# Token sums and split y made ahead one operation a step, parked in DRAM and read back on GpSimd's queue; the low half of h one projection later

## The chip, the cores and the metric

The kernel runs on one core of a Trainium2 chip. The metric is device time in microseconds (us). The engines are called PE (TensorE, the matmuls), PEld (its weight loads), DVE (VectorE), ACT (ScalarE), POOL (GpSimd) and SP (SyncE, which here issues DMAs).

## What is computed

The reference, cut to what matters. Attention with random features comes first; two MLPs follow, and the change lies in these alone.

```python
x = attention(q, k, v, omega)            # 4 x 576 tokens -> x of 2304 x 512
# kind 1 (SwiGLU), d_ff = 1536
xn = x / rms(x) * rms_g
x = (silu(xn @ w_gate) * (xn @ w_val)) @ w_out
# kind 2, d_ff = 2048
x = silu(x @ w_in) @ w_out2
```

The weights come in as 64-bit floats, read as pairs of 32-bit words.

## The kernel before

Tokens lie in five blocks: 0 to 3 of 512, block 4 of 256. Every fp32 operand is kept as a high and a low half in the fast matmul type (fp32r): ACT writes the high half (a copy), DVE the low half (operand minus high), and each product is three matmul passes (high x high, high x low, low x high). xs[j] holds the split activations of block j, in four chunks of 128 channels; ya[j] its sums y in fp32; a `w_tile` slot holds a split weight.

The hidden dimension is cut into f-blocks of 128, 12 in kind 1 and 16 in kind 2. Blocks 0, 1 and 4 are done in **sweeps** of two f-blocks each: `g1_glu` (kind 1) projects gate and value, multiplies them (L254), and `split_h` makes the two halves of h (L224 on ACT, L225 on DVE); `g2_glu` adds the y product to ya (L285, L296) while the next block's projections run. `n1` is the last kind-1 sweep, `n2` the last of kind 2. In kind 2 `g1_mlp` has one projection and no product, and `g2_mlp` (L318, sums L329) makes y.

Blocks 2 and 3 are done in **quads**, by a scheme that takes 7 block products in place of 8 (L483), 10 quads of one f-block in kind 1 and 8 of two in kind 2. They need four sums of token blocks, T1 to T4, split and laid into parts of xs: T1 and T2 in xs[0], T3 in xs[1], T4 in xs[3], which are free once the sweeps have been through. They need sums of weight blocks too (`sums`, L442 to L445), and splits of those (`pieces`, `split`, low half at L359). `pieces` for quad k+1 and `out_pieces` for quad k's output weight go out during quad k, one group of at most two operations a step, from the list `todo`. Kept fp32 weights come back from DRAM by `load` and `load_out`.

Before the quads of a kind, the T work (`t_value`, L377; low half at L359, high at L401) goes out in the last sweep, after `flush` has emptied the list; POOL does T3 in kind 1. After the last kind-1 quad, `split_y` writes the y of blocks 0 and 1, split, to xs[0] and xs[1] for kind 2 (ACT L562, DVE L359), while the last `both` (y of blocks 2 and 3) runs: its own splits stand at L275.

The weights are prepared along the way: `Prep.tick` loads one weight (L155 to L166 are five DVE operations, L169 two POOL additions, L173 ACT's high half, L176 DVE's low half), and `need` ticks on until a weight is there. The lists of weights to prepare are extended in `hook`, per sweep.

Code runs in the order in which `stream` yields steps; each engine has its own queue and takes its instructions in that order. SP issues the DMAs in order too.

Of the kernel before, what the change touches and what calls it, by code (L numbers as in the profile page):

```python
# [20 lines left out]
def kernel(  # L21
# [345 lines left out]
    def t_value(kind, nm, k, eng):  # L367


        def b(r, c):  # L370
# [1012 lines left out]
```

## Time and profile before

| | us |
|---|---|
| median of 3 runs (1035.70 to 1037.78) | 1036.72 |
| profiled execution | 1036.71 |
| span in the profile | 1034.6 |
| PE busy | 1000.7 |
| DVE busy | 775.7 |
| ACT busy | 438.2 |
| POOL busy | 352.9 |

The profile is of one execution; times in it count from the start of the span. The mean granted clock of the span was 0.985 of 2.4 GHz. Where the granted clock of a stretch is below 1.00, PE ran a part of it at 1.2 GHz. An operation's time in a timeline is its own duration; the distance from one start to the next on an engine is shorter where operations overlap by some hundredths.

### The profile page before, as it was taken

To read this page: it belongs to the slowest core of one execution; us is meant where nothing else is said; L and a number is where in the kernel's file an instruction comes from. 1 tells how busy PE (TensorE), PEld (TensorE's weight loads), DVE (VectorE), ACT (ScalarE), POOL (GpSimd) and SP (SyncE) were. 2 spreads that over 40 slices of the span, in tenths; PEclk is the share of its full clock that TensorE was granted. 3 is DMA by queue.
4 is the path that set the end of the run, shared out by engine and by line. 5 is a ranking of instruction groups with operands and counts; after the bars stand their busy time and mean duration, and the time that the engine had idled before them with its cause. 6 is when DMAs were issued, how large, how long until landed. Compare 5 with 4: busy or idle time off the path is not lost.

```text
span 1034.6 us, 14957 instructions
## 1 busy us (share of the span) xinstructions
PE 1000.7 (97%) x5315; PEld 850.4 (82%) x5315; DVE 775.7 (75%) x1579; ACT 438.2 (42%) x991; POOL 352.9 (34%) x365
## 2 busy tenths in 40 slices
PE   8999999999999999988999987999999998999998
PEld 7999998888888888776888765788888886788877
DVE  6899999534767768887777875799977658576675
ACT  6888886433222212134332334433323235533441
POOL 7656644312434434512122230545434302121100
PEclk9999999999999999988999998999999999999999
DMA  7353221212425324101111230444433213221102
GB/s 186 100 156 91 75 62 43 92 37 76 123 92 150 95 92 137 38 21 61 52 41 61 84 121 1 122 148 129 151 112 107 89 41 102 63 69 52 41 21 82
DMA packets 86586, 88.33 MB, mean 85 GB/s; under 512 B 27632, under 2 KB 64752, under 8 KB 86512
## 3 DMA queue, kind: packets, MB, share of 16 engines
q1 hardware_dynamic: 86512, 87.38, 28.2%
q8 instruction: 42, 0.69, 0.3%
q14 instruction: 32, 0.26, 0.1%
HBM read 66.39 MB, written 20.97 MB: 84 GB/s over the span
## 4 chain that ended last, share of the span: by engine, by line
PE 80%; DVE 14%; ACT 4%; issue 2%; DMA 0%; SPq 0%; DVEq 0%; ACTq 0%
PE g L231 22%; PE y L318 17%; PE g L483 11%; PE y L285 10%; PE b L906 5%; PE b L231 3%; PE kv L989 3%; PE b L1034 2%; DVE s L377 2%; PE b L887 2%; PE b L1261 2%; PE b L1020 1%; DVE h L225 1%; DVE w L359 1%; DVE s L362 1%
## 5 line engine op out<-in xcount | busy, mean ns | idle before, releaser
L169 POOL TENSOR_TENSOR m<-m,raw 128x512 int32<-128x512 int32 x136 | 188.9, 1389 | 315.6 <-DVE m L166 304.0
L231 PE MATMUL g<-xs,w 128*128 128x512 f32 (+1 forms) x1392 | 276.4, 356 | 8.3 <-DVE s L254 6.1
L231 PEld LDWEIGHTS g<-xs,w 128*128 128x128 f32 x1392 | 232.2, 191 | 48.2 <-DVE s L254 6.3
L318 PE MATMUL y<-w,h 128*128 128x512 f32 (+1 forms) x870 | 207.7, 395 | 8.0 <-ACT h L224 4.4
L318 PEld LDWEIGHTS y<-w,h 128*128 128x128 f32 x870 | 163.9, 191 | 46.1 <-ACT h L224 5.2
L225 DVE TENSOR_TENSOR h<-s,h 128x512 fp32r<-128x512 f32 (+1 forms) x134 | 102.7, 774 | 115.7 <-ACT h L224 115.6
L483 PE MATMUL g<-xs,w 128*128 128x512 f32 x756 | 182.4, 400 | 6.9 <-DVE s L362 5.3
L483 PEld LDWEIGHTS g<-xs,w 128*128 128x128 f32 x756 | 144.1, 192 | 42.6 <-DVE s L362 8.1
L285 PE MATMUL y<-h,w 128*128 128x512 f32 (+1 forms) x648 | 138.5, 370 | 3.0 <-DVE ya L296 2.8
L285 PEld LDWEIGHTS y<-h,w 128*128 128x128 f32 x648 | 112.9, 190 | 25.5 <-DVE ya L296 4.7
L224 ACT ACTIVATE h<-s 128x512 fp32r<-128x512 f32 (+1 forms) x134 | 78.0, 587 | 120.7 <-DVE s L254 77.3
L329 DVE TENSOR_TENSOR ya<-y,ya 128x512 f32<-128x512 f32 (+1 forms) x127 | 84.4, 681 | 21.3 <-PE y L318 20.9
L173 ACT ACTIVATE w<-m 128x512 fp32r<-128x512 f32 x68 | 43.0, 632 | 130.3 <-POOL m L169 130.2
L442 POOL TENSOR_TENSOR w<-w 128x256 f32<-128x256 f32 x18 | 15.9, 884 | 238.2 <-DMA w<-kept1v 91.4
L945 ACT ACTIVATE e<-b,nb 128x128 f32<-128x128 f32 x272 | 77.5, 386 | 8.8 <-DVE nb L934 8.5
L176 DVE TENSOR_TENSOR w<-m,w 128x512 fp32r<-128x512 f32 x68 | 67.8, 997 | 4.2 <-ACT w L173 4.0
L296 DVE TENSOR_TENSOR ya<-y,ya 128x512 f32<-128x512 f32 (+1 forms) x100 | 60.4, 630 | 14.0 <-PE y L285 14.0
L906 PE MATMUL b<-bd,hl 128*128 128x256 f32 x432 | 69.5, 299 | 0.4 <-DVE hl L896 0.3
L362 DVE TENSOR_TENSOR s<-s,g 128x512 f32<-128x512 f32 x90 | 61.3, 681 | 9.7 <-PE g L483 9.2
L359 DVE TENSOR_TENSOR w<-w,w 128x512 fp32r<-128x512 f32 (+1 forms) x98 | 65.6, 683 | 0.6 <-ACT w L455 0.5
L906 PEld LDWEIGHTS b<-bd,hl 128*128 128x128 f32 x432 | 56.9, 194 | 1.7 <-DVE hl L896 0.6
L921 DVE TENSOR_REDUCE small<-b 128x4 f32<-128x512 f32 x72 | 50.1, 695 | 5.8 <-PE b L906 3.3
(96 smaller groups left out, 1131.0 us busy)
## 6 DMA issues: line engine op xcount, KB each, us to landing
raw<-in_moe_w_out_dram SPq DMA_DIRECT2D x28, 512.0 KB, 4.0
raw<-in_moe_w_in_dram SPq DMA_DIRECT2D x16, 512.0 KB, 4.2
raw<-in_moe_w_gate_dram SPq DMA_DIRECT2D x12, 512.0 KB, 4.0
raw<-in_moe_w_val_dram SPq DMA_DIRECT2D x12, 512.0 KB, 4.0
x<-in_k_dram SPq DMA_DIRECT2D x16, 256.0 KB, 3.3
va<-in_v_dram SPq DMA_DIRECT2D x32, 128.0 KB, 3.3
x<-in_q_dram SPq DMA_DIRECT2D x16, 256.0 KB, 3.0
kept2i<-m SPq DMA_DIRECT2D x16, 256.0 KB, 4.2
```

The lines of the kernel that those rows point to most:

```text
L169: tt(out=mi, in0=mi, in1=(low if step == 5 else high).bitcast(I32), op=ALU.add)
L224: nc.scalar.activation(out=ht[:, 0, :], in_=s, func=AF.Copy)
L225: nc.vector.tensor_tensor(out=ht[:, 1, :], in0=s, in1=ht[:, 0, :].bitcast(F32), op=ALU.subtract)
L231: nc.tensor.matmul(out=ps, lhsT=w[:, a, cc * P:(cc + 1) * P], rhs=xs[j][:, c, cc, :], start=(n == 0), stop=(n == 3 * KC - 1),)
L285: nc.tensor.matmul(out=ps, lhsT=wt[1, "o", f][:, a, d * P:(d + 1) * P], rhs=hs[f][:, c, :], start=(n == 0), stop=(n == nn - 1),)
L318: nc.tensor.matmul(out=ps, lhsT=hs[f][:, a, t * P:(t + 1) * P], rhs=wt[2, "p", f][:, c, d0:d1], start=(n == 0), stop=(n == nn - 1),)
L329: nc.vector.tensor_tensor(out=o[:, t, d0:d1], in0=ps, in1=o[:, t, d0:d1], op=ALU.add)
L359: nc.vector.tensor_tensor(out=out, in0=a, in1=b, op=ALU.subtract)
L362: nc.vector.tensor_tensor(out=out, in0=a, in1=b, op=ALU.add)
L483: nc.tensor.matmul(out=ps, lhsT=self.t[n][:, w, o:o + P], rhs=rhs(b, c)[:, k, :], start=start and m == 0 and k == 0, stop=stop and m == 2 ...
L906: nc.tensor.matmul(out=st.ps[:, 2 * j:2 * j + 2, :].rearrange("p h m -> p (h m)"), lhsT=st.hl[:, c, j, :], rhs=bd[:, a, :], start=(n == 0) ...
L945: nc.scalar.activation(out=st.e[:, h, :], in_=st.ps[:, h, :], func=AF.Exp, bias=st.nb[:, h:h + 1])
```

## The change

What it does:

- `split_h` gives ACT its copy and puts DVE's low subtract in a list, `owed`; `settle` issues it after the next projection.
- T1, T2 and T3 are computed in an earlier sweep (sweep 2 of kind 1 by its number, n1 + 2 of kind 2, and the one behind it), one operation a step on DVE, split into a weight slot and written to DRAM by SP (`park`); `t_load` reads them into xs in the last sweep, with DMAs issued on POOL's queue. T4 is written directly.
- `split_y` is gone. `y_jobs` splits one chunk of ya[0] or ya[1] in each of the quads 1 to 8, parks it, and `y_load` reads all eight back on POOL's queue after quad 9 (512 KB each).
- The weight sums go from POOL to DVE.
- `pieces` are given out in two lists with the next `load` between them; `out_pieces` of quad 0 go ahead with the first pieces; the ring of output slots has three entries in place of four.
- In kind 2, silu of z comes before the y stretch and not after it.
- A low half of the fourth chunk that `g2_glu` wrote in the last kind-1 sweep, with no high half to it (L275), is left out.
- The weights of sweep n1 + 2 are added to the list after the last kind-1 quad, not in sweep n1 + 1.

The core of the diff:

```diff
 def split_h(s, j):
     nc.scalar.activation(out=ht[:, 0, :], in_=s, func=AF.Copy)
-    nc.vector.tensor_tensor(out=ht[:, 1, :], in0=s, in1=ht[:, 0, :].bitcast(F32), op=ALU.subtract)
+    owed.append(lambda: nc.vector.tensor_tensor(
+        out=ht[:, 1, :], in0=s, in1=ht[:, 0, :].bitcast(F32), op=ALU.subtract
+    ))
     return ht
+def settle():
+    while owed:
+        owed.pop(0)()
 ...
     yield from proj(wt[1, "g", f], j, p)
+    settle()
 ...
+def park(key, slot, value):
+    t, v = [], []
+    def high():
+        v.append(value())
+        t.append(w_tile(*slot))
+        nc.scalar.activation(out=t[0][:, 0, :], in_=v[0], func=AF.Copy)
+    def low():
+        dsub(t[0][:, 1, :], v[0], t[0][:, 0, :].bitcast(F32))
+        parked[key] = cache.tile([P, 2, TB * P], F32, name="parked_%s%d%d" % key)
+        nc.sync.dma_start(out=parked[key], in_=t[0].bitcast(F32))
+    return [high, low]
+def unpark(key, out):
+    nc.gpsimd.dma_start(out=out, in_=parked[key])
+def t_load(kind, *names):
+    for nm in names:
+        j, h = RHS[nm]
+        for k in range(2):
+            unpark((nm, kind, k), xs[j][:, :, 2 * h + k, :])
+def y_load():
+    for j in (0, 1):
+        for d in range(KC):
+            unpark(("y", j, d), xs[j][:, :, d, :])
 ...
-    self.oslots = [[(1, 7), (1, 8), (1, 4), (1, 5)][k % 4]]
+    self.oslots = [[(1, 7), (1, 8), (1, 4)][k % 3]]
 ...
 def sums(self):
-    tt = nc.gpsimd.tensor_tensor
+    tt = nc.vector.tensor_tensor
 ...
 def hook(si, j, n):
+    if si == (2 if kind == 1 else n1 + 2):
+        todo.extend(t_jobs(kind, ((1, 6), (1, 7), (1, 8)) if kind == 1 else ((1, 8), (1, 7), (1, 5))))
 ...
     if at == (0, 0):
+        flush(todo)
         q.load()
         q.load_out()
     elif at == (0, 1):
-        jobs = [e for k in range(2) for nm in ("T1", "T2") for e in t_jobs(kind, nm, k, vec)]
-        todo.extend(groups(jobs) + groups(q.pieces() + [quads[kind, 1].load]))
+        t_load(kind, "T2", "T1")
+        a, b = q.pieces()
+        todo.extend(groups(a + [quads[kind, 1].load] + b + q.out_pieces()))
     elif at == (1, 1):
-        flush(todo)
-        ...
+        t_load(kind, "T3")
 ...
+    jobs = [lambda: None] * (4 if pend else 0)
     if k + 1 < count:
-        jobs += quads[kind, k + 1].pieces()
-    if k + 2 < count:
-        jobs.append(quads[kind, k + 2].load)
-    jobs += q.out_pieces()
+        a, b = quads[kind, k + 1].pieces()
+        jobs += a + ([quads[kind, k + 2].load] if k + 2 < count else []) + b
+    if k:
+        jobs += q.out_pieces()
     ...
+    if k and ys:
+        a, b = ys.pop(0)
+        todo += [[a], [b]]
 ...
-    if kind == 1:
-        pend = along(pend, [[lambda j=j, d=d: split_y(j, d)] for j in (0, 1) for d in range(KC)])
+    if kind == 2:
+        settle()
+    else:
+        prep.jobs += prep_list(n1 + 2)
+        y_load()
```

How DVE's row reads in sweep 3 of kind 1, block 0, before: L254 is the product of gate and value, L225 the low half of h, L176 a weight's low half, L155 to L166 the decoding of another weight, L296 a y sum.

```order
L254 TENSOR_TENSOR s<-s,g 128x512
L225 TENSOR_TENSOR h<-s,h 128x512
L176 TENSOR_TENSOR w_5_4538<-m_4493,w_5_4538 128x512
L155 TENSOR_SCALAR m_4577<-raw_4540 128x512
L158 TENSOR_SCALAR raw_4540<-raw_4540 128x512
L161 TENSOR_SCALAR m_4577<-m_4577 128x512
L163 TENSOR_SCALAR raw_4540<-raw_4540 128x512
L166 TENSOR_SCALAR m_4577<-m_4577 128x512
L296 TENSOR_TENSOR ya_95<-y,ya_95 128x512 x3
```

And after, where the lines are L264 (product), L228 (low half of h), L307 (y sum) and L370 (here the low half of a parked T sum, made in w_8):

```order
L264 TENSOR_TENSOR s<-s,g 128x512
L176 TENSOR_TENSOR w_5_4573<-m_4524,w_5_4573 128x512
L155 TENSOR_SCALAR m_4617<-raw_4575 128x512
L158 TENSOR_SCALAR raw_4575<-raw_4575 128x512
L161 TENSOR_SCALAR m_4617<-m_4617 128x512
L163 TENSOR_SCALAR raw_4575<-raw_4575 128x512
L166 TENSOR_SCALAR m_4617<-m_4617 128x512
L370 TENSOR_TENSOR w_7_4577<-w_8_4485,w_7_4577 128x512
L228 TENSOR_TENSOR h<-s,h 128x512
L307 TENSOR_TENSOR ya_95<-y,ya_95 128x512
```

The low half of h stood directly behind its product, and stands now behind a weight's low half, five decode operations and a parked low half.

DVE in the last kind-1 sweep ahead of the first quad, before (L377 are T sums, L359 their low halves, the product L254 last):

```order
L377 TENSOR_TENSOR s<-s,xs_93 128x512
L377 TENSOR_TENSOR s<-s,xs_92 128x512
L296 TENSOR_TENSOR ya_95<-y,ya_95 128x512
L359 TENSOR_TENSOR xs_90<-s,xs_90 128x512
L377 TENSOR_TENSOR s<-xs_93,xs_90 128x512
L377 TENSOR_TENSOR s<-s,xs_93 128x512
L377 TENSOR_TENSOR s<-s,xs_90 128x512
L275 TENSOR_TENSOR xs_90<-ya_95,xs_90 128x512
L359 TENSOR_TENSOR xs_90<-s,xs_90 128x512
L254 TENSOR_TENSOR s<-s,g 128x512
```

And after (L370 are low halves of quad 0's weight pieces, L264 the product):

```order
L307 TENSOR_TENSOR ya_95<-y,ya_95 128x512
L370 TENSOR_TENSOR w_0_5400<-w_4_5345,w_0_5400 128x512
L307 TENSOR_TENSOR ya_95<-y,ya_95 128x512
L370 TENSOR_TENSOR w_1_5426<-w_4_5345,w_1_5426 128x256
L307 TENSOR_TENSOR ya_95<-y,ya_95 128x512
L370 TENSOR_TENSOR w_2_5448<-w_5_5395,w_2_5448 128x512
L307 TENSOR_TENSOR ya_95<-y,ya_95 128x512
L370 TENSOR_TENSOR w_3_5459<-w_5_5395,w_3_5459 128x512
L370 TENSOR_TENSOR w_7_5463<-w_6_5348,w_7_5463 128x512
L264 TENSOR_TENSOR s<-s,g 128x512
```

The T4 sums are gone from here, and low halves of weights stand between the y sums.

DVE in the y stretch after the last kind-1 quad, before (L359 are the subtracts of `split_y`, L275 the low halves of block 2's own y):

```order
L296 TENSOR_TENSOR ya_97<-y,ya_97 128x512
L359 TENSOR_TENSOR xs_90<-ya_95,xs_90 128x512
L296 TENSOR_TENSOR ya_97<-y,ya_97 128x512
L275 TENSOR_TENSOR xs_92<-ya_97,xs_92 128x512
L359 TENSOR_TENSOR xs_90<-ya_95,xs_90 128x512
L296 TENSOR_TENSOR ya_97<-y,ya_97 128x512
L275 TENSOR_TENSOR xs_92<-ya_97,xs_92 128x512
L359 TENSOR_TENSOR xs_90<-ya_95,xs_90 128x512
L296 TENSOR_TENSOR ya_97<-y,ya_97 128x512
L275 TENSOR_TENSOR xs_92<-ya_97,xs_92 128x512
L176 TENSOR_TENSOR w_2_6834<-m_6790,w_2_6834 128x512
```

And after:

```order
L307 TENSOR_TENSOR ya_97<-y,ya_97 128x512 x2
L286 TENSOR_TENSOR xs_92<-ya_97,xs_92 128x512
L307 TENSOR_TENSOR ya_97<-y,ya_97 128x512
L286 TENSOR_TENSOR xs_92<-ya_97,xs_92 128x512
L307 TENSOR_TENSOR ya_97<-y,ya_97 128x512
L286 TENSOR_TENSOR xs_92<-ya_97,xs_92 128x512
L176 TENSOR_TENSOR w_2_6893<-m_6842,w_2_6893 128x512
L155 TENSOR_SCALAR m_6952<-raw_6895 128x512
L158 TENSOR_SCALAR raw_6895<-raw_6895 128x512
L161 TENSOR_SCALAR m_6952<-m_6952 128x512
L163 TENSOR_SCALAR raw_6895<-raw_6895 128x512
L166 TENSOR_SCALAR m_6952<-m_6952 128x512
```

The `split_y` subtracts between the y sums are gone; the decoding of a further weight stands there. The loads that bring the split y back stand on POOL's row, after, between the additions of two weights:

```order
L169 TENSOR_TENSOR m_6842<-m_6842,raw_6797 128x512 x2
L398 DMA xs_90<-parked_y_5833 128x2x512
L398 DMA xs_90<-parked_y_5954 128x2x512
L398 DMA xs_90<-parked_y_6089 128x2x512
L398 DMA xs_90<-parked_y_6210 128x2x512
L398 DMA xs_91<-parked_y_6345 128x2x512
L398 DMA xs_91<-parked_y_6466 128x2x512
L398 DMA xs_91<-parked_y_6601 128x2x512
L398 DMA xs_91<-parked_y_6723 128x2x512
L169 TENSOR_TENSOR m_6952<-m_6952,raw_6895 128x512 x2
```

All eight loads stand behind the additions of the weight that is decoded in the last quad and ahead of those of the next weight; before, POOL's row has no DMA.

## Rows read from the trace of the kernel before

**Rows 1.** the view of stretches, most of both MLPs

```profile
core 0: us, PE busy (x) PEld busy (x) DVE busy (x) ACT busy (x) POOL busy (x), PEclk, DMA share, GB/s
215.00:430.00 215.00, 215.00 (x1111) 183.85 (x1110) 143.14 (x281) 57.42 (x103) 77.53 (x58) 1.00 0.32 98
430.00:500.00 70.00, 61.15 (x276) 50.53 (x275) 58.88 (x89) 23.85 (x47) 22.26 (x22) 0.90 0.13 42
500.00:600.00 100.00, 99.81 (x435) 80.99 (x434) 76.34 (x124) 34.31 (x64) 22.18 (x25) 1.00 0.20 62
600.00:680.00 80.00, 68.41 (x278) 53.22 (x277) 57.56 (x98) 32.95 (x59) 22.88 (x16) 0.91 0.25 80
680.00:850.00 170.00, 168.84 (x811) 140.69 (x810) 135.74 (x236) 53.23 (x97) 64.45 (x48) 1.00 0.37 113
850.00:900.00 50.00, 46.39 (x199) 36.59 (x197) 33.70 (x53) 27.79 (x52) 11.54 (x12) 0.97 0.27 86
```

**Rows 2.** PE's waits, 430 to 500: who, for whom, us, times, longest

```profile
PE g L231 <- DVE s L254: 6.1, 1, 6.1
```

**Rows 3.** timeline, T sums on DVE and POOL: start, us, operation

```profile
427.22 1.42 DVE L377 TENSOR_TENSOR s<-s,xs 128x512 f32<-128x512 f32 x2
431.49 3.31 POOL L377 TENSOR_TENSOR s<-s,xs 128x512 f32<-128x512 f32 x2
431.99 3.36 DVE L377 TENSOR_TENSOR s<-s,xs 128x512 f32<-128x512 f32 x2
```

**Rows 4.** PE's waits, 600 to 680 us

```profile
PE y L318 <- ACT h L224: 4.1, 1, 4.1
PE y L285 <- DVE ya L296: 2.6, 3, 0.9
PE g L483 <- DVE s L362: 2.4, 1, 2.4
PE g L231 <- DVE w L176: 2.2, 1, 2.2
```

**Rows 5.** DVE by line, 600 to 640: busy us, mean ns, idle before

```profile
L359 DVE TENSOR_TENSOR xs<-ya,xs 128x512 fp32r<-128x512 f32 x8 | 5.5, 689 | 4.3 <-ACT xs L562 4.3
```

**Rows 6.** timeline of POOL, 646 to 650, idle before in brackets

```profile
648.09 3.01 POOL L169 TENSOR_TENSOR m<-m,raw 128x512 int32<-128x512 int32 x2 [34.54 <-DVE m L166]
```

**Rows 7.** PE's waits, 850 to 900 us

```profile
PE y L318 <- DVE w L359: 2.4, 1, 2.4
```

**Rows 8.** timeline in sweep 3, from L254 to the y product

```profile
337.12 0.69 DVE L254 TENSOR_TENSOR s<-s,g 128x512 f32<-128x512 f32 x1 [2.87 <-PE g L231]
338.51 0.69 DVE L225 TENSOR_TENSOR h<-s,h 128x512 fp32r<-128x512 f32 x1 [0.70 <-ACT h L224]
339.12 0.68 DVE L176 TENSOR_TENSOR w<-m,w 128x512 fp32r<-128x512 f32 x1
339.65 5.63 PE L285 MATMUL y<-h,w 128*128 128x512 f32 x24
339.72 0.42 DVE L155 TENSOR_SCALAR m<-raw 128x512 uint32<-128x512 uint32 x1
341.06 0.42 DVE L166 TENSOR_SCALAR m<-m 128x512 uint32<-128x512 uint32 x1
```

**Rows 9.** timeline of DVE, a half-width operation and the next

```profile
480.15 0.42 DVE L359 TENSOR_TENSOR w<-w,w 128x256 fp32r<-128x256 f32 x1
480.49 0.68 DVE L362 TENSOR_TENSOR s<-s,g 128x512 f32<-128x512 f32 x1
```

**Rows 10.** the timeline of PE, a pair of quads

```profile
501.56 19.52 PE L483 MATMUL g<-xs,w 128*128 128x512 f32 x84
```

**Rows 11.** DMA issues: count, KB each, median us to landing

```profile
raw<-in_moe_w_out_dram SPq DMA_DIRECT2D x28, 512.0 KB, 4.0
```

More of the change, by code (lines that the diff above doesn't have):

```diff
@@ L301, in g2_glu @@
             yield nn * blocks[j] / 2365
-        if last:
+        if last and last[0] < KC:
             low(KC - 1)
@@ new lines, in unpark, with t_jobs, b, op @@
+    def unpark(key, out):
+        nc.gpsimd.dma_start(out=out, in_=parked[key])
+    def t_jobs(kind, slots):
+        jobs = []
+        for k in range(2):
+            def b(r, c, k=k):
+                n = 2 * r - 2 + k
+                if kind == 1:
+                    return [xs[c + 1][:, w, n, :].bitcast(F32) for w in range(2)]
+                return [ya[c + 1].rearrange("p (c t) -> p c t", c=KC)[:, n, :]]
+            v = {}
+            def op(n, first, alu, a, c, v=v):
+                def run():
+                    if first:
+                        v["t"] = w_tile(*slots[2], F32)
+                    t = v["t"]
+                    x, y = [t[:, e, :] if isinstance(e, int) else e for e in (a, c)]
+                    nc.vector.tensor_tensor(out=t[:, n, :], in0=x, in1=y, op=alu)
+                return run
+            def ops(n, plus, minus, first=False):
+                out = [op(n, first, ALU.subtract, plus[0], minus[0])]
+                out += [op(n, False, ALU.add, n, a) for a in plus[1:]]
+                return out + [op(n, False, ALU.subtract, n, a) for a in minus[1:]]
+            def t4_high(v=v, k=k):
+                nc.scalar.activation(out=rhs("T4", 0)[:, k, :], in_=v["t"][:, 1, :], func=AF.Copy)
+            def t4_low(v=v, k=k):
+                dsub(rhs("T4", 1)[:, k, :], v["t"][:, 1, :], rhs("T4", 0)[:, k, :].bitcast(F32))
+            p1, p2, p3 = [
+                park((nm, kind, k), slots[n % 2], lambda n=n, v=v: v["t"][:, n % 2, :])
+                for n, nm in enumerate(("T1", "T2", "T3"))
+            ]
+            seq = ops(0, b(1, 2), b(1, 1), True) + ops(1, b(2, 2), [0]) + [p1[0], p2[0], p1[1], p2[1]]
+            seq += ops(0, b(2, 2), b(1, 2)) + ops(1, b(2, 1), [1]) + [p3[0], t4_high, p3[1], t4_low]
+            jobs += [[e] for e in seq]
+        return jobs
@@ L490, in product, with half_h, silu @@
                     )
+    def half_h(hs, f, j, v):
+        hs[j][f] = split_h(v, j)
+    def silu(out, in_):
+        nc.scalar.activation(out=out, in_=in_, func=AF.Silu)
     def quad_set(q, hs, pend, late, todo):
         cost = 6 * TB * P / 2365
+        f0, f1 = q.fs[0], q.fs[-1]
         def step(c):
@@ L517, in quad_set @@
         dadd(z, z, e)
+        if q.kind == 2:
+            silu(z, z)
         yield step(cost)
@@ L621, in hook @@
         def hook(si, j, n):
[L622 removed]
+            kind = sweeps[si][0]
             if (j, n) == (H1[2] if si == n1 + 1 else H1[0], 0):
[L624 to L626 removed]
+                s = si + (1 if si < n1 else 2)
+                if si != n1 and s <= n2:
+                    prep.jobs += prep_list(s)
+                if si == (2 if kind == 1 else n1 + 2):
+                    todo.extend(t_jobs(kind, ((1, 6), (1, 7), (1, 8)) if kind == 1 else ((1, 8), (1, 7), (1, 5))))
             if si not in (n1, n2):
```

93 lines of the change are left out of this document (33 added, 60 removed).

## The prediction

> **What bounds the kernel now.** The first view is the table of stretches [rows 1]: one row for each part of the two MLPs, with TensorE's (PE's) busy time and granted clock. The reader is to see that PE is full and at 2.4 GHz (granted clock 1.00) in the kind-1 sweeps (215 to 430 us), in the kind-1 quads (500 to 600) and nearly so in the kind-2 sweeps (680 to 850), and that it loses time in three short places. I count the loss of a stretch as its idle time plus (1 - granted clock) x its busy time, since 0.90 is a mean of stretches at 2.4 and at 1.2 GHz: 430 to 500 loses 8.85 + 0.10 x 61.15 = 15.0 us; 600 to 680 loses 11.59 + 0.09 x 68.41 = 17.7; 850 to 900 loses 3.61 + 0.03 x 46.39 = 5.0; 680 to 850 loses 1.2 and 500 to 600 loses 0.2. So PE is the bound, and about 39 us of waits, with the low clock that follows the waits, are all that a change of order can win. No matmul is added, removed or moved.
>
> The second view, PE's waits, names the causes. In 430 to 500 PE waits 6.1 us for VectorE's (DVE's) L254, the product silu x value of the last sweep [rows 2]. It came late because the T3 and T4 sums (L377) stand ahead of it, and GpSimd (POOL) runs its T3 sums at the same time: two DVE sums take 3.36 us beside two POOL sums of 3.31, and 1.42 alone [rows 3]. In 600 to 680 PE waits 4.1 us for h, 2.6 for the ya sums, 2.4 for L362 and 2.2 for a weight's low half, L176 [rows 4]. The eight split_y subtracts on DVE (5.5 us) stand between the ya sums there [rows 5], and POOL begins the decoding of the weight that L176 ends only at 648.09, after 34.54 us in which nothing was asked of it [rows 6]. In 850 to 900 it is 2.4 us for the low half of an out weight, L359 [rows 7].
>
> **The change part by part.** All sums are made against the profiled execution, 1036.71 us (span 1034.6), which is the median of the runs shown, 1036.72.
>
> First transition, 430 to 500. The T work leaves it: the flush goes, T1 to T3 come from DRAM, and POOL has no T3 sums, so nothing is left ahead of L254 but one subtract of 0.7. Following DVE's new order through quads 0 and 1 at the intervals below, I find one late sum of about 0.4 us; I leave 0.8. Gain 15.0 - 0.8 = 14.2. The six loads are issued in the last sweep, several us ahead.
>
> Second transition, 600 to 680. The eight subtracts and their ACT copies go, and the preparation of the second kind-2 sweep begins a stage earlier, which removes the L176 wait. What is late next: the low half of the last h stands behind five prep operations (about 1.9 us for the block-4 y), the first y of block 2 waits for the low half of its h (about 1.3), and A22 x T4 about 0.6. Gain 17.7 - 3.8 = 13.9. The y loads must be there when block 0 is projected, about 25.4 us after quad 9 begins: 9.8 us of quad (84 matmuls of two quads in 19.52 [rows 10]), two y stretches and block 4. POOL comes to them, in its order behind the adds of the fourth weight, about 12.8 us after quad 9 begins. Before has no load on POOL's queue. The nearest rows: 512 KB on SP's queue land in 4.0 us [rows 11], and 113 GB/s at a DMA share of 0.37 [rows 1] make some 305 GB/s at full share, or 1.7 us for 512 KB, so the first four land about 12.8 + 2.3 + 4 x 1.7 = 21.9, 3.5 us ahead. One after the other at 4.0 each they would end at 28.8, 3.4 us late. I take 0, the overlapped value, since the SP rows show several transfers sharing the engines, and keep 3.4 for the range.
>
> Third transition, 850 to 900. The out pieces come a quad later with a weight slot of their own and POOL's weight sums no longer hold them up: 5.0 - 0.7 = 4.3.
>
> Kind-2 sweeps, 680 to 850. DVE is already busy 135.74 of 170 [rows 1]; T work of two sweeps is added. The 1.2 us lost there stays or goes with the low halves; I take 1.2 back and 3.0 new (0 to 5), net -1.8.
>
> Kind-1 sweeps. These lose nothing now. The low half of the second h moves behind what stands after it in DVE's row, because it is emitted after the next projection. In the old order the product starts at 337.12, the low half at 338.51 and ends at 339.20; y starts at 339.65, 2.53 us after the product [rows 8]. Its fifth matmul is the first to read this low half, four matmuls of about 0.21 later: the limit is 3.38 us after the product. A two-input 128x512 operation costs an interval of 0.60 (338.51, 339.12, 339.72), a decode operation 0.335 (339.72 to 341.06 is four) [rows 8]. With five decode operations ahead the end is 0.60 + 1.68 + 0.69 = 2.97, in time; with a weight low half too it is 3.57, 0.2 to 0.3 late; with a parked piece's low half besides (the order of sweep 3 in the section on the change) 4.17, 0.8 late, and the same again if one of these meets POOL's adds as in [rows 3]: 1.65 each. Six such places: 0.3, 0.3, 0.3, 1.65, 1.65, 0.6 with the small ones of sweep 2, or 4.8 us (2 to 8). Below 2 it is only if DVE ran ahead, above 8 only if every place met POOL.
>
> Quads. The weight sums move from POOL to DVE: four 128x256 operations, at 0.34 each (480.15 to 480.49 [rows 9]) to 0.52 beside POOL, 1.4 to 2.1 us a quad. An odd quad then has 14 full and 5 half operations, 14 x 0.60 + 5 x 0.34 = 10.1 us, against 9.76 of PE; an even one has the y stretch to recover in. About 0.3 us for each of five odd quads, 1.7 us with the even ones (0 to 5). DVE now waits for the kept weights' loads with all its work behind it: they are issued in step 3 of a quad and read at the start of the next, four products or some 5.5 us later, and 512 KB land in 4.0, so I price this at nothing; without that cover it would be 1 to 2 us a quad.
>
> **The sum**: 14.2 + 13.9 + 4.3 - 1.8 - 4.8 - 1.7 = 24.1 us; 1036.7 - 24.1 = 1012.6. The ends of the unknown costs: 2, 0 and 0 for sweeps, quads and kind-2 sweeps give 1005; 8, 5, 5 and the 3.4 of the loads give 1024.
>
> **The rivals.** (1) DVE becomes the bound. It goes to some 85% busy in the sweeps with T work: 143.14 of 215 now [rows 1], and 28 more operations of 0.60 in two sweeps. POOL is busy there 36% of the time (77.53 of 215); if so many of the 28 take 1.68 in place of 0.7 us [rows 3], that is 28 x 0.36 x 1 = 10 us, and with 2 us more in the quads the time is 1024. For it: that collision. Against: in [rows 8] DVE runs at its lone speed, and the sums are one a step, not a burst.
>
> (2) Slower than before: the loads on POOL's queue crawl. Eight loads of 512 KB are in that queue, block 0 waits for the first four, block 1, some 34.5 us after quad 9 begins, for all. If they come one at a time, the delay for L us each is 12.8 + 8L - 34.5: it begins at L = 2.7 and eats the 24.1 us won at L = 5.8; at 7 us it is 34.3, and the time 1047. For it: no load was ever issued from that queue here, POOL shares something with DVE [rows 3], and DVE is nearly always busy at that place. Against: 4.0 us for 512 KB on the other queue, and T loads with a longer lead. The Trainium skill, page "SBUF — State Buffer", section "SBUF: two separate sides", says that descriptors of a transfer issued from GpSimd are written by GpSimd itself, and that a DVE operation in its two-port mode locks it out meanwhile; by that rule these eight loads would be the ones held up, and 12.8 would grow by whatever DVE runs without a gap. No run of before shows such a load; that DVE and POOL stretch each other, [rows 3] agrees.
>
> (3) None of the new waits in the sweeps, quads and kind-2 sweeps appears, because DVE has run ahead: the sum without 1.8, 4.8 and 1.7 is 32.4, and 1.2 more, so 1003.
>
> (4) It doesn't do what it says: the late work returns at the same places (a slot of the parking still read, a load that holds the queue), and the gains cancel: 1036.
>
> **How the numbers follow.** Forecast 0.57 (1005 to 1021), rival 1 0.20 (1024), rival 3 0.09 (1003), rival 2 0.09 (1047), rival 4 0.05 (1036). The time is the forecast's, 1012.6. The range 1002 to 1026 takes in the forecast, rivals 1 and 3, and leaves out 0.14. About 2 us (0.2%) is what a measurement tells from no change. Faster: 0.57 + 0.20 + 0.09 = 0.86; same: most of rival 4, 0.04; slower: 0.10.
>
> **What would show it.** Right: in the profile after, the waits for L254, split_y's subtracts and the out weight's low half are gone and the granted clock of the three transitions is 1.00 or close to it; small waits of y for h's low half appear in sweep 3, of 1 to 2 us. Rival 1: DVE over 95% busy in the sweeps with T work, and its two-input operations well over 0.7 us there. Rival 2: PE waits for a DMA into xs before block 0 or 1 of the first kind-2 sweep. Wrong altogether: a new half-clock stretch in the sweeps, where a wait of mine would cost twice itself.

## The result and the profile after

The changed kernel takes 1047.82 us (median of 4 runs, 1046.91 to 1050.75) against 1036.34 for the kernel before: ratio 1.0114, 95% interval 1.0091 to 1.0137. The change makes the kernel some 11 us slower; 24 us faster was forecast, and the time lies outside the range.

The view of stretches of the profile after, with the columns and the times of [rows 1] (what is computed at 680 us is by then some us later than before):

```profile
core 0: us, PE busy (x) PEld busy (x) DVE busy (x) ACT busy (x) POOL busy (x), PEclk, DMA share, GB/s
215.00:430.00 215.00, 200.83 (x1019) 169.84 (x1018) 156.10 (x283) 56.25 (x103) 77.09 (x52) 0.98 0.34 107
430.00:500.00 70.00, 68.13 (x330) 56.69 (x330) 45.10 (x86) 23.37 (x45) 7.38 (x9) 0.98 0.31 94
500.00:600.00 100.00, 98.17 (x425) 79.18 (x425) 83.96 (x151) 38.53 (x70) 0.00 (x0) 1.00 0.29 95
600.00:680.00 80.00, 73.66 (x313) 58.74 (x312) 69.87 (x121) 32.94 (x58) 44.19 (x32) 0.96 0.57 175
680.00:850.00 170.00, 158.86 (x739) 130.57 (x739) 139.79 (x226) 50.07 (x92) 59.87 (x40) 0.97 0.36 114
850.00:900.00 50.00, 50.00 (x232) 41.59 (x231) 31.92 (x57) 22.77 (x44) 4.27 (x6) 1.00 0.51 158
```

Lost time counted as in the prediction (idle, plus (1 - granted clock) x busy) gives:

| stretch (us) | before | after | after, as predicted |
|---|---|---|---|
| 215 to 430, kind-1 sweeps | 0.0 | 18.2 | 4.8 |
| 430 to 500, first transition | 15.0 | 3.2 | 0.8 |
| 500 to 600, kind-1 quads | 0.2 | 1.8 | 1.9 |
| 600 to 680, second transition | 17.7 | 9.3 | 3.8 |
| 680 to 850, kind-2 sweeps | 1.2 | 15.9 | 3.0 |
| 850 to 900, third transition | 5.0 | 0.0 | 0.7 |

The clock is given to 0.01, so a loss in a stretch of 200 us is known to about 1 us. The three transitions give back 25.2 us, not far from the 32.4 forecast. The sweeps, which lost next to nothing before, now lose 34 us, and that takes all of it and more. PE's waits over the whole span of after (who, for whom, us in total, times, longest) name what is late:

```profile
PE y L329 <- DVE h L228: 13.8, 8, 4.5
PE y L296 <- DVE h L228: 10.5, 7, 4.1
PE g L537 <- DVE s L373: 4.6, 2, 2.8
PE y L296 <- ACT h L227: 3.6, 2, 2.0
...
PE y L296 <- DVE ya L307: 2.5, 4, 0.6
```

L228 is the low half of h, the operation that the change postpones; L227 is its high half on ACT. The waits for L254, for a weight's L176 and for an out weight's L359 ([rows 2, 4, 7]) are gone, as the change means them to be.

What one such place looks like: sweep 3 of the changed kernel, block 1, the timeline of DVE, then of POOL, then of PE (start, us, engine, line). L264 is the product, L228 the low half that y's fifth matmul reads:

```profile
366.81 0.68 DVE L264 TENSOR_TENSOR s<-s,g 128x512 f32<-128x512 f32 x1
367.41 1.20 DVE L176 TENSOR_TENSOR w<-m,w 128x512 fp32r<-128x512 f32 x1
368.65 1.41 DVE L155 TENSOR_SCALAR m<-raw 128x512 uint32<-128x512 uint32 x1
...
371.32 0.68 DVE L370 TENSOR_TENSOR w<-w,w 128x512 fp32r<-128x512 f32 x1
371.93 1.76 DVE L228 TENSOR_TENSOR h<-s,h 128x512 fp32r<-128x512 f32 x1
...
366.43 3.35 POOL L169 TENSOR_TENSOR m<-m,raw 128x512 int32<-128x512 int32 x2 [3.69 <-DVE m L166]
371.54 3.30 POOL L169 TENSOR_TENSOR m<-m,raw 128x512 int32<-128x512 int32 x2 [1.76 <-DVE m L166]
...
373.74 2.76 PE L296 MATMUL y<-h,w 128*128 128x512 f32 x6 [4.07 <-DVE h L228]
```

The order is the one that the prediction counted for this place (a weight's low half, five decode operations, a parked low half), and it was to end 4.17 us after the product. It ends 6.88 us after (366.81 to 373.69), because L176 takes 1.20 in place of 0.68, L155 1.41 in place of 0.43 and L228 1.76 in place of 0.68. All three stand beside one of POOL's two pairs of additions (L169). PE waits 4.07 us.

### The profile page after: what moved, and what is told of

It is laid out like the page before. It is cut to its first block, busy times and chain, and to the rows that moved or that the text cites. A ratio compares the mean times of both kernels' runs of the same rounds, so it can differ in the third digit from the quotient of the medians.

```text
span 1045.1 us, 14956 instructions
## 1 busy us (share of the span) xinstructions
PE 1001.8 (96%) x5315; PEld 850.4 (81%) x5315; DVE 808.0 (77%) x1647; ACT 438.0 (42%) x991; POOL 309.8 (30%) x307
## 4 chain that ended last, share of the span: by engine, by line
PE 72%; DVE 20%; issue 3%; DMA 2%; ACT 2%; SPq 1%; POOL 0%; DVEq 0%; POOLq 0%
PE g L240 18%; PE y L329 17%; PE g L537 10%; PE y L296 8%; PE b L974 5%; PE b L240 3%; PE kv L1057 3%; DVE h L228 2%; PE b L1102 2%; DVE w L370 2%; DVE s L373 2%; DVE m L155 2%; PE b L1329 2%; DVE ya L307 2%; PE b L1088 1%
## 5 line engine op out<-in xcount | busy, mean ns | idle before, releaser
L169 POOL TENSOR_TENSOR m<-m,raw 128x512 int32<-128x512 int32 x136 | 203.3, 1495 | 456.8 <-DVE m L166 425.7
L329 PE MATMUL y<-w,h 128*128 128x512 f32 (+1 forms) x870 | 209.5, 397 | 13.9 <-DVE h L228 13.8
L329 PEld LDWEIGHTS y<-w,h 128*128 128x128 f32 x870 | 164.6, 192 | 52.7 <-DVE h L228 18.2
L537 PE MATMUL g<-xs,w 128*128 128x512 f32 x756 | 180.2, 397 | 4.8 <-DVE s L373 4.6
L296 PE MATMUL y<-h,w 128*128 128x512 f32 (+1 forms) x648 | 142.9, 375 | 16.6 <-DVE h L228 10.5
L296 PEld LDWEIGHTS y<-h,w 128*128 128x128 f32 x648 | 114.4, 194 | 41.9 <-DVE h L228 13.7
L227 ACT ACTIVATE h<-s 128x512 fp32r<-128x512 f32 (+1 forms) x134 | 78.0, 587 | 148.7 <-DVE s L264 103.3
L228 DVE TENSOR_TENSOR h<-s,h 128x512 fp32r<-128x512 f32 (+1 forms) x134 | 109.6, 827 | 23.4 <-ACT h L227 22.4
L340 DVE TENSOR_TENSOR ya<-y,ya 128x512 f32<-128x512 f32 (+1 forms) x127 | 86.7, 684 | 51.5 <-PE y L329 50.6
L373 DVE TENSOR_TENSOR s<-s,g 128x512 f32<-128x512 f32 x90 | 61.4, 682 | 30.4 <-PE g L537 27.3
L370 DVE TENSOR_TENSOR w<-w,w 128x512 fp32r<-128x512 f32 (+1 forms) x110 | 73.9, 680 | 10.1 <-ACT w L509 10.1
L307 DVE TENSOR_TENSOR ya<-y,ya 128x512 f32<-128x512 f32 (+1 forms) x100 | 61.7, 630 | 21.1 <-PE y L296 21.0
L276 ACT ACTIVATE s<-g 128x512 f32<-128x512 f32 (+1 forms) x48 | 25.0, 522 | 102.1 <-PE g L240 102.1
L176 DVE TENSOR_TENSOR w<-m,w 128x512 fp32r<-128x512 f32 x68 | 62.8, 923 | 5.3 <-ACT w L173 5.1
L509 ACT ACTIVATE w<-w 128x512 fp32r<-128x512 f32 (+1 forms) x98 | 52.8, 582 | 10.1 <-DVE w L497 9.9
```

Of the source, the lines that this page charges most:

```text
L169: tt(out=mi, in0=mi, in1=(low if step == 5 else high).bitcast(I32), op=ALU.add)
L228: owed.append(lambda: nc.vector.tensor_tensor(out=ht[:, 1, :], in0=s, in1=ht[:, 0, :].bitcast(F32), op=ALU.subtract))
L296: nc.tensor.matmul(out=ps, lhsT=wt[1, "o", f][:, a, d * P:(d + 1) * P], rhs=hs[f][:, c, :], start=(n == 0), stop=(n == nn - 1),)
L307: nc.vector.tensor_tensor(out=y[:, d, :], in0=ps, in1=y[:, d, :], op=ALU.add)
L329: nc.tensor.matmul(out=ps, lhsT=hs[f][:, a, t * P:(t + 1) * P], rhs=wt[2, "p", f][:, c, d0:d1], start=(n == 0), stop=(n == nn - 1),)
L340: nc.vector.tensor_tensor(out=o[:, t, d0:d1], in0=ps, in1=o[:, t, d0:d1], op=ALU.add)
```

## The experiments

Each kernel was timed beside the kernel before on the same chip. Medians in us; the ratio is to that kernel before, whose medians in the four groups of runs were 1035.69, 1035.03, 1035.86 and 1035.01.

| run | what differs | us | ratio (95% interval) |
|---|---|---|---|
| e1_low_at_once | the change, low half of h at once | 1039.48 | 1.0033 (1.0019 to 1.0046) |
| e2_before_low_later | kernel before, low half later | 1039.93 | 1.0037 (1.0024 to 1.0049) |
| e3_no_pool_adds | the change, no POOL additions | 1020.29 | 0.9843 (0.9819 to 0.9867) |
| e4_sums_pool | the change, weight sums on POOL | 1042.05 | 1.0059 (1.0039 to 1.0078) |
| e5_park_step_later | the change, stores a step later | 1042.52 | 1.0066 (1.0049 to 1.0083) |
| e6_sweeps_at_once | e5, low half at once in sweeps | 1029.42 | 0.9946 (0.9931 to 0.9961) |
| e7_with_pool_sums | e6, weight sums on POOL | 1022.69 | 0.9880 (0.9865 to 0.9894) |
| e8_no_token_sums | the change, no token sums | 1017.83 | 0.9831 (0.9817 to 0.9846) |
| e9_t2_without_prep | e7, kind-2 sums moved | 1014.72 | 0.9797 (0.9780 to 0.9813) |
| e10_t_without_prep | e9, kind-1 sums moved too | 1011.61 | 0.9765 (0.9750 to 0.9780) |
| e11_change_t_moved | the change, all token sums moved | 1041.93 | 1.0066 (1.0049 to 1.0082) |
| e12_low_later_again | e10, low half later in sweeps | 1025.51 | 0.9906 (0.9888 to 0.9924) |

**e1: the postponed low half undone.**

```diff
-        owed.append(lambda: nc.vector.tensor_tensor(
-            out=ht[:, 1, :], in0=s, in1=ht[:, 0, :].bitcast(F32), op=ALU.subtract
-        ))
+        nc.vector.tensor_tensor(out=ht[:, 1, :], in0=s, in1=ht[:, 0, :].bitcast(F32), op=ALU.subtract)
```

> The changed kernel with one thing undone: the low half of h is subtracted at once, directly behind its high half. Theory 1 (the postponed low half is what costs): in the changed kernel PE waits 10.5 + 13.8 us for it and then runs some stretches at 1.2 GHz, about 34 us in the two groups of sweeps; most of that goes, some 28 us, and the time is about 1020 (1012 to 1026). Theory 2 (the token-sum work fills DVE in the sweeps, whatever order it is given in): less than half goes, 1034 or more, and the wait of y for the low half of h is over 10 us in all still.

Measured 1039.48, 8.3 us better than the change and still slower than before. That is theory 2's number, and its other sign is there too: PE still waits 12.1 us for L228, and 9.5 for the high half L227 (3.6 in the change), since DVE is late with the product. So the postponement is a part of the cost, and the smaller one in this form. What is left can be read in the largest wait, 7.6 us in front of y at 704.70. Here is what stands ahead of it, on DVE, and on SP (PE's line last):

```profile
699.16 0.43 DVE L155 TENSOR_SCALAR m<-raw 128x512 uint32<-128x512 uint32 x1 [2.49 <-DMA kept2i<-m]
...
703.15 1.50 DVE L228 TENSOR_TENSOR h<-s,h 128x256 fp32r<-128x256 f32 x1
...
695.50 0.32 SPq L391 DMA_DIRECT2D parked_T<-w  x1
...
697.17 0.63 SPq L182 DMA_DIRECT2D kept2i<-m  x1
...
704.70 1.22 PE L327 MATMUL y<-w,h 128*128 128x512 f32 x2 [7.57 <-DVE h L228]
```

DVE stands 2.49 us for the store of a decoded weight (kept2i), whose buffer L155 writes next, and everything behind L155 stands too; then five decode operations, a parked low half, a y sum and a token sum (1.18 us) come before the low half, which takes 1.50 for 256 columns.

**e2: the postponed low half alone, on the kernel before.** The same `owed` and `settle` as in the change, in the kernel before, and nothing else.

> The kernel before with this one part of the change alone: the low half of h is subtracted after the next projection. No token sums in the early sweeps, weight sums on POOL, split_y as before. Theory 1 (the postponed low half costs by itself, behind a weight's preparation): about 2 us for each kind-1 sweep and 0.5 to 1 for each kind-2 sweep, 1044 (1040 to 1050). Theory 2 (it costs only together with the token-sum work): 1035 to 1038.

1039.93, 4.2 us more than before, just below theory 1's lower bound. The 4.2 us are a net figure. The sweeps lose 9.5 us more than before: 3.7 in 215 to 430, by places of 0.3 us (blocks of 512 tokens) and 1.3 us (block 4), and 7.0 in 680 to 850 (1.2 before), by five places of 1.2 to 1.4 and two below 0.4. The three transitions lose 31.9 in place of 37.7, so 5.8 less. In all PE waits 17.2 us for the low half here, and 1.4 in the kernel before.

**e3: no additions on POOL.**

```diff
-            tt(out=mi, in0=mi, in1=(low if step == 5 else high).bitcast(I32), op=ALU.add)
+            pass
```

The decode operations ahead of it get other constants, and one another input (cut here), so that the weights are other finite numbers; their count and kind stay.

> The changed kernel without the two POOL additions per weight (L169); the decoding's constants are changed so that the weights are other finite numbers, with the same count and kind of DVE, ACT and PE work. Theory 3 (POOL's additions start when L166 ends, just when the postponed low half of h, a DVE operation with two SBUF inputs, comes up, and stretch it from 0.69 to 1.76 us): the 15 or so late low halves come 1 to 2 us sooner each and the half-clock stretches behind them go, about 1030 (1022 to 1036). Against it: the wait is the work ahead alone, and the time is within 4 us of the changed kernel's 1047.8.

1020.29, 27.5 us better, and 2 us below the band: theory 3's direction, and more than its size. (Leaving the additions out takes away the collision and also the time that ACT's high half waits for them; this run doesn't part the two.) This is the same place as above, in this kernel, DVE and then PE:

```profile
358.63 0.69 DVE L264 TENSOR_TENSOR s<-s,g 128x512 f32<-128x512 f32 x1 [1.02 <-PE g L240]
359.23 0.68 DVE L176 TENSOR_TENSOR w<-m,w 128x512 fp32r<-128x512 f32 x1
359.95 0.43 DVE L155 TENSOR_SCALAR m<-raw 128x512 uint32<-128x512 uint32 x1
...
361.77 0.68 DVE L370 TENSOR_TENSOR w<-w,w 128x512 fp32r<-128x512 f32 x1
362.37 0.68 DVE L228 TENSOR_TENSOR h<-s,h 128x512 fp32r<-128x512 f32 x1
...
363.11 3.24 PE L296 MATMUL y<-h,w 128*128 128x512 f32 x13 [0.83 <-DVE h L228]
```

The same operations, now at 0.68, 0.43 and 0.68: the low half ends 4.42 us after the product (358.63 to 363.05; the prediction said 4.17), and PE waits 0.83, as the prediction said (0.8) for a place that meets no addition. The view of stretches:

```profile
215.00:430.00 215.00, 210.48 (x1082) 178.01 (x1080) 144.72 (x302) 58.63 (x111) 3.07 (x4) 1.00 0.37 116
...
680.00:850.00 170.00, 166.80 (x791) 139.32 (x790) 115.17 (x226) 53.51 (x101) 4.27 (x6) 0.99 0.41 130
```

The kind-1 sweeps lose 4.5 us by the idle time, nearly the 4.8 of the prediction, the kind-2 sweeps 3.2 and 1.7 more of low clock.

**e4: the weight sums back on POOL.** In `sums`, `tt = nc.gpsimd.tensor_tensor`.

> The changed kernel with the weight sums of the quads back on POOL. Theory 4 (the four sums of 128x256 on DVE make each odd quad late): what is lost from 430 to 600 us in the changed kernel (about 5 us) goes and the time is 1043 to 1045. Against it: POOL's sums meet DVE's low halves and are slower themselves, and the out weights come late again as before (2.4 us): 1047 to 1052. Theory 1 expects no more than 5 us either way.

1042.05, 5.8 us better, a bit more than the bound of theory 4. In 430 to 600 us the loss falls from 5.0 to 1.7 (0.9 idle in the first stretch, 0.8 in the second, granted clock 1.00 in both); most of the rest lies at 600 to 680, where the clock is 1.00 in place of 0.96; it is 1.00 in e1 and e5 too, with the sums on DVE, so that this part is due to the sums isn't shown. Moving these sums to DVE cost 5.8 us by this run, where the prediction had 1.7 (0 to 5). Out weights didn't come late with the sums on POOL (850 to 900 us are full here too); the other edits, out pieces a quad later among them, may have cured that, but none was undone alone.

**e5: a parked tile's store one step later.** The DMA that `low` in `park` issues goes into a list that is emptied at the start of the next step:

```diff
-            nc.sync.dma_start(out=parked[key], in_=t[0].bitcast(F32))
+            to_ship.append(lambda: nc.sync.dma_start(out=parked[key], in_=t[0].bitcast(F32)))
```

> The changed kernel, with only the store of a parked tile issued one step later, so that SP doesn't stand waiting for the tile's low half with other stores behind it. Theory 5 (SP's wait holds up the store of a decoded weight, kept<-m, and DVE's next decoding, L155, waits for that store with all of DVE behind it): DVE's waits for kept stores fall from 9.3 us in all to about 1, and 5 to 10 us of the time go with them, 1040 (1037 to 1043). Against it: PE's waits for the low half of h stay and the time is 1046 or more.

1042.52, 5.3 us better, inside theory 5's band, but not by its mechanism: DVE's waits for kept stores hardly fall. They were (DVE's waits, after first, then e5):

```profile
DVE m L155 <- DMA kept2i<-m: 5.4, 3, 2.0
...
DVE m L155 <- DMA kept1g<-m: 2.1, 2, 1.5
...
DVE m L155 <- DMA kept2p<-m: 1.8, 2, 1.0
```

```profile
DVE m L155 <- DMA kept2i<-m: 5.4, 3, 2.1
...
DVE m L155 <- DMA kept2p<-m: 2.0, 2, 1.2
...
DVE m L155 <- DMA kept1g<-m: 0.4, 1, 0.4
...
DVE m L155 <- DMA kept1v<-m: 0.2, 1, 0.2
```

That is 9.3 against 8.0, where about 1 was expected; before they were 0.8 in all. SP's wait does hold up kept stores at one place that the changed kernel's timeline shows (SP stands 2.06 us for two parked tiles, the store of kept1g goes out behind them, L155 waits 1.49):

```profile
309.76 2.06 SPq L393 DMA_DIRECT2D parked_T<-w  x2
311.88 0.42 SPq L182 DMA_DIRECT2D kept1g<-m  x1
...
315.27 0.43 DVE L155 TENSOR_SCALAR m<-raw 128x512 uint32<-128x512 uint32 x1 [1.49 <-DMA kept1g<-m]
```

But e8, which parks no token sums at all, keeps 4.8 us of such waits, so a part of them has another cause. POOL's additions, which come ahead of the store, don't explain it alone: e3, which has none, keeps 7.0.

**e6: e5, and the low half at once in the sweeps.** `split_h` calls `settle` itself, except for the quads.

> As the run with the store one step later, and the low half of h subtracted at once in the sweeps (in the quads still later, as in the changed kernel). Theory 1 and 5 together (two causes that add): the undone postponement gave 8 us, so 1040 - 8 = 1032 (1028 to 1036). If they are one cause seen twice: no more than 2 us better than the better of the two alone, 1037 to 1040.

1029.42, inside the band: 18.4 us better than the change, where 8.3 (e1) and 5.3 (e5) make 13.6. Beside e5 the postponement is worth 13.1 us, not the 8.3 of e1. e1 had also undone it in the quads, where it helps: there 500 to 600 us lose 4.5 us, and here 2.5. And DVE's waits for kept stores, 9.3 in the change, are 8.6 in e1 and 8.0 in e5, but 1.8 here: they go only with both parts undone.

**e7: e6, and the weight sums on POOL.**

> As the run before it, and the quads' weight sums back on POOL, which alone gave 6 us: 1026 (1022 to 1031) if that gain adds; it would then beat the kernel before. If POOL's sums only help where the postponed low half is late, 1032.

1022.69, 6.7 us better than e6, as e4 had promised, and now faster than the kernel before by 1.2%.

**e8: no token sums.** The lines that add `t_jobs` and call `t_load` are taken out; the quads then multiply what lies in the tiles of T1 to T4.

> The changed kernel with the token sums T1 to T4, their parking and their loads left out (the quads read what lies in those tiles). Theory 2 (the token-sum work in the sweeps is what makes the low half late): the stalls of sweeps 2 and 3 of both kinds go, some 25 us with their half clock, 1022 (1018 to 1028). If the postponement costs by itself, as in the run on the kernel before, 5 us of stalls stay in the sweeps of each kind; if it is all of the cost, the time is 1040 or more.

1017.83, 30 us better, 0.2 below theory 2's band. The stretches:

```profile
215.00:430.00 215.00, 211.74 (x1091) 179.83 (x1090) 139.90 (x276) 58.28 (x106) 75.38 (x54) 1.00 0.32 98
...
680.00:850.00 170.00, 168.60 (x803) 140.17 (x802) 131.15 (x213) 53.38 (x98) 51.96 (x36) 1.00 0.31 100
```

3.3 and 1.4 us are lost in the sweeps, with the clock at 1.00, although the low half is postponed here as in the change. So with the additions alone (e8) the sweeps lose 4.7 us, with the token sums alone (e3) 9.4, and with both, in a row where the low half comes last, 34. (e8 leaves out the token sums' stores and loads too.)

**e9: e7, with the kind-2 token sums in sweep n2 - 1**, where no weight is decoded and POOL adds nothing but one pair at the start (794.27):

```diff
-                if si == (2 if kind == 1 else n1 + 2):
+                if si == (2 if kind == 1 else n2 - 1):
-                    todo.extend(t_jobs(kind, ... else ((1, 8), (1, 7), (1, 5))))
+                    todo.extend(t_jobs(kind, ... else ((0, 0), (0, 3), (1, 8))))
```

> The fastest version so far (store a step later, low half at once in the sweeps, weight sums on POOL) with one thing moved: the kind-2 token sums start in sweep n2 - 1, where no weight is prepared any more and POOL makes no additions. The same work goes beside the same matmuls, but not beside POOL's additions. Theory 6 (the token sums cost because they stand beside POOL's additions): the stalls of the first kind-2 sweeps (5.3 us idle and about 3 of low clock from 680 to 850) go to 1 or 2, none come later, and the time is 1016 (1014 to 1018). If it is the amount of DVE work a sweep, the stalls move with the sums and the time stays at 1021 to 1024.

1014.72, 8.0 us better, and theory 6's number. The stretch 680 to 850 loses 0.8 us (e7: 5.3 idle and 0.02 of clock) with the same sums, no later stretch loses more:

```profile
680.00:850.00 170.00, 164.73 (x777) 137.38 (x776) 126.52 (x222) 54.69 (x101) 62.42 (x50) 0.98 0.42 130
```

```profile
680.00:850.00 170.00, 169.16 (x807) 140.96 (x806) 128.31 (x227) 57.07 (x107) 58.34 (x49) 1.00 0.43 137
```

**e10: e9, and the kind-1 token sums moved too**, two operations a step from block 4 of sweep n1 - 1 on, with the loads after block 1 of the last sweep:

```diff
+            if si == n1 - 1 and (j, n) == (H1[2], 0):
+                todo.extend([a[0], b[0]] for a, b in (lambda t: zip(t[::2], t[1::2]))(t_jobs(1, ((1, 6), (1, 7), (1, 8)))))
...
+                elif at == (1, 1):
+                    flush(todo)
+                    t_load(1, "T2", "T3", "T1")
```

> As the run before it, and the kind-1 token sums too: two operations a step from the last block of sweep 4 on, through the last kind-1 sweep, where POOL makes no additions; the loads of T1 to T3 go out after block 1 of the last sweep, and quad 0's pieces after them. Theory 6: the 12 us of the kind-1 sweeps (8.3 idle, the rest low clock) go to 2; against that stand 0 to 5 us of new waits ahead of quads 0 and 1, where the pieces are crowded and the loads land late: 1008 (1004 to 1013). If the amount of DVE work decides, sweep 5 stalls as sweeps 2 and 3 did and the time is 1016 or more.

1011.61, 3.1 us better than e9 and inside the band; this is the fastest kernel of the study, 2.35% faster than the one before. Not all of the sweeps' 12 us went: 3.8 us idle and 0.02 of clock are left in 215 to 430, by one wait of 3.8 us at 412.82 in the part of sweep n1 - 1 where the sums run two a step. The expectation took it that POOL makes no additions there; this place still meets a pair (DVE, with L427 the token sums, then POOL, then PE):

```profile
407.89 3.37 DVE L427 TENSOR_TENSOR w<-w,xs 128x512 f32<-128x512 f32 x2
...
407.39 3.32 POOL L169 TENSOR_TENSOR m<-m,raw 128x512 int32<-128x512 int32 x2 [2.49 <-DVE m L166]
...
412.82 5.10 PE L298 MATMUL y<-h,w 128*128 128x256 f32 x21 [3.80 <-ACT h L227]
```

The product stands behind these sums in DVE's row, and the high half of h (L227) waits for the product.

**e11: the change as given, with the token sums moved as in e10 and nothing else.**

> The changed kernel as it was given, with only the token sums moved to where POOL makes no additions (as in the last two runs); the low half of h later, the stores in SP's row and the weight sums on DVE all as in the change. Theory 6: most of the 34 us lost in the sweeps was the token sums beside POOL's additions, so some 22 us go, 1025 (1019 to 1031), of which 3 to 5 us of postponed low halves and a crowded start of the quads remain. Theory 1 or 5 (the postponed low half or SP's stores by themselves): no more than 10 us go, 1038 or more.

1041.93: 5.9 us better, not the 22 that theory 6 expected, but the number of theories 1 and 5. In the sweeps that keep only the decoding, single waits are 0.3 to 1.3 us, as in e8; the large ones now stand where the sums went (2.25 and 1.60 us up to 418.06, 1.85 and 1.07 up to 439.55, 5.37 at 852.51), with stretches below 2.4 GHz behind them (granted clock 0.62 from 415.95 to 425). The first of these places still meets a pair of additions, as in e10. The largest on DVE:

```profile
845.42 0.68 DVE L228 TENSOR_TENSOR h<-s,h 128x512 fp32r<-128x512 f32 x1
850.30 0.42 DVE L496 TENSOR_TENSOR w<-w 128x256 f32<-128x256 f32 x1 [4.19 <-DMA w<-kept2i]
...
851.77 0.68 DVE L228 TENSOR_TENSOR h<-s,h 128x512 fp32r<-128x512 f32 x1
```

A weight sum on DVE stands 4.19 us for a kept weight's load, and the postponed low half of h, behind it in the row, with it. The prediction named this wait and priced it at nothing (for a load of 512 KB, where a kept weight has 256 KB). In the change itself no such wait shows; it comes here, where the new order brings the load later.

**e12: e10 with the low half postponed in the sweeps again.**

> The fastest version (token sums away from POOL's additions, store a step later, weight sums on POOL) with the low half of h postponed in the sweeps again, as the change has it. Theory 1 in its smaller form (the postponement costs what it cost on the kernel before, 4 us): 1015.5 (1013 to 1019). If it costs only together with token sums beside POOL's additions: within 2 us of 1011.6.

1025.51: 13.9 us, over three times what theory 1 expected from e2, and neither theory's number. PE waits 14.5 us for L228 over the whole span, against 0.7 in e10, and 1.6 for L227 against 5.4. Its waits from 680 to 850 us, of e10 and then of e12:

```profile
PE y L331 <- ACT h L227: 0.8, 1, 0.8
```

```profile
PE y L329 <- DVE h L228: 3.4, 6, 1.3
```

3.4 us in that stretch, by six places of 0.3 to 1.3. The others are 3.2 us in the kind-1 sweeps with decoding alone, 4.3 in the second transition (3.1 of them at 641.81), and 3.6 where the token sums stand two a step ahead of the postponed low half (2.2 at 415.95, beside a pair of additions, and 1.4 at 437.31), with the clock below 1.00 from 415.95 to 425 (0.70, then 0.56).

**What the runs settle, and what not.**

- A low half of h that is postponed is late by what DVE is given in the meantime. With decoding alone PE's waits for it come to 17.2 us on the kernel before (e2); the time shows 4.2 of them, since the transitions lose less there. In e12, where most token sums are away from the additions, they come to 14.5, 5.6 of it at places with token sums, and the time shows 13.9.
- In a row with both the token sums and POOL's additions it is worst, since the additions begin when L166 ends and meet what stands next. Without the additions (e3) 9.4 us of the change's 34 are left in the sweeps, without the token sums (e8) 4.7, so the two shares overlap and can't be added.
- Moving the sums gives 11 us where the low half is subtracted at once (e7 to e10) and only 6 where it is postponed (e11). But e11 also keeps the weight sums on DVE and the stores at once, so it isn't shown that the postponement alone makes this difference.
- DVE's waits for kept stores fall only with the store a step later and the low half at once: 1.8 us in e6 and 2.1 in e10, against 9.3 in the change, 8.6 in e1, 8.0 in e5 and 6.2 in e12. By which way isn't isolated.

## Why the prediction was wrong, step by step

- **Kind-1 sweeps, -4.8 us (2 to 8): measured 18.2.** This is the step that failed, with the next one. The mechanism was the right one (a limit of 3.38 us after the product, or 3.47 at the 5.63 / 24 = 0.23 us a matmul of [rows 8], and what stands ahead of the low half), and e3 shows the working near the truth where no POOL addition is met: 4.42 for 4.17 us, 4.5 us in all for 4.8. The mis-sized part is the collision. It was given to two of six places, one operation each, at some 0.85 us, where [rows 3] give 0.97; and the upper bound said "only if every place met POOL". Of PE's nine waits for h in this stretch (14.1 us), eight stand behind at least one DVE operation that an addition stretches; at 352.74 none is stretched, and the wait is 0.61, near the 0.8 counted. The meeting isn't chance: the additions start when L166 ends, and what follows L166 in DVE's row runs beside them. At 373.74 not one but three operations are stretched (L176, L155, L228), for 4.07 us. Two of the nine waits, 3.6 us, had no term at all: they are for the high half L227, since its product itself stood late behind stretched operations.
- **Kind-2 sweeps, -1.8 us net: measured -14.7.** The same term; no place was walked through there at all, and "3.0 new (0 to 5)" was a guess from a busy share. Two waits of 4.47 and 3.64 us, behind token sums and low halves beside additions and an L155 that stood for a kept store, make most of it. e9 shows that with the low half at once the sums cost next to nothing at another place (0.8 us lost).
- **Low clock.** Behind the longest of the late low halves PE ran at 1.2 GHz for some 3 to 5 us each (granted clock 0.60 from 373.7 to 378, 0.50 from 693.2 to 698, 0.60 from 707.7 to 712, after 4.07, 4.47 and 3.64 us without work). The prediction said that this would double its waits and put no term for it into the sum; it is some 4.0 of the 18.2 and 4.8 of the 15.9.
- **First transition, gain 14.2: 11.8.** Right in kind; a late L373 of 1.8 us in quad 1, for 0.4 counted, with 1.4 of low clock. It is there in e8 too (1.8), and 0.4 in e4 and e7: it comes with the weight sums on DVE.
- **Second transition, gain 13.9: 8.4.** The split y loads were in time, no PE wait for them shows. What was late were L373 in the last quad (2.8; it was 2.4 before [rows 4], and the prediction had 0.6) and a low half of h behind an L155 that stood 2.0 us for a kept store (2.7), with low clock. The earlier preparation of sweep n1 + 2 put more decoding there, 44 us of POOL against 23 before [rows 1].
- **Third transition, gain 4.3: 5.0**, right. **Quads, -1.7: -1.6** in 500 to 600, right by luck: the waits there are for ya sums (0.6 each) and not for L373, and e4 shows that the whole move of the sums cost 5.8.
- **Rival 1** (DVE becomes the bound) had the cause, token sums beside POOL, and the wrong price: 10 us from chance meetings, where leaving out the sums gives 30 (e8). Its sign of DVE over 95% busy didn't come (156.10 of 215 us, 139.79 of 170); its sign of two-input operations well over 0.7 us did. **Rival 2** gave the sign and not the mechanism: eight loads on POOL's queue land in 9.2 us (median), but side by side, and no wait of PE for them shows. (By its own formula the gain is eaten at L = 5.7, not 5.8.) Rivals 3 and 4 didn't come.

In short: the gains were read rightly from the waits of before; the costs were walked through at DVE's lone speed, though [rows 3] in the prediction showed the other one.

## What to carry to other kernels

When an operation is put later in an engine's row, count not the gap that it fills but everything that the row holds between its operand and its reader, at the speed that these have beside the other engine that is released by the same row. Work spread one piece a step isn't free in a stretch that has no slack after the reader's limit; put it where the colliding engine rests (8.0 us in e9). A part that costs 4 us by itself can cost 14 in another kernel, since the 4 can be the net of a larger loss and a gain (e2, e12). Undo parts one at a time: this change held a gain of 25 us in its three transitions, and with two of its parts taken back (the low half in the sweeps, the weight sums) and two moved (the stores, the token sums) it is 2.35% faster than the kernel before.

## What the runs showed of the hardware

POOL's pair of additions and DVE slow each other when DVE's operands are in SBUF: 1.76 us for 0.68 with two such inputs, 1.41 for 0.43 for L155 with one. The pair takes 3.30 to 3.36 us then, and 2.70 at 405.02 in after, most of it beside y sums, which read PSUM. An operation with one input in PSUM isn't stretched: all 90 of L373 in after take 0.67 to 0.69 us. Here three of them, the first two started inside a pair of additions, take 2.26 us in a row, in the last kind-1 quad of after (POOL, then DVE):

```profile
615.59 3.30 POOL L169 TENSOR_TENSOR m<-m,raw 128x512 int32<-128x512 int32 x2 [3.69 <-DVE m L166]
...
615.97 1.77 DVE L370 TENSOR_TENSOR w<-w,w 128x512 fp32r<-128x512 f32 x1
617.67 2.26 DVE L373 TENSOR_TENSOR s<-s,g 128x512 f32<-128x512 f32 x3
```

The Trainium skill, page "SBUF — State Buffer", section "SBUF: two separate sides", says that DVE and GpSimd share one pair of ports under an exclusive lock, taken for a whole instruction by a DVE operation with two SBUF inputs (against a GpSimd operation that reads SBUF) or in a two-port mode. These rows agree: 1.77 with two SBUF inputs, and no stretch with one in PSUM; in which mode L155 ran no run here shows. The Trainium skill, same page and section, also says that a DVE operation in its two-port mode starves transfers issued from GpSimd's queue, which would make the loads of split y slow. They are slower than loads of the same size on SP's queue, 5.8 and 9.2 us against the 4.0 of [rows 11], but two to four (T) and eight (y) were issued in a row, and no run separates the two causes:

```profile
xs<-parked_T POOLq DMA_DIRECT2D x12, 512.0 KB, 5.8
...
xs<-parked_y POOLq DMA_DIRECT2D x8, 512.0 KB, 9.2
```
